# A Fourier mixing and low-rank mixer kernel on one core: one sum of the second batch's fold taken in the opening, one of the third batch's loads issued after the second batch's narrow sums, and the third batch's fold three slots later

## The chip, the core and the metric

The kernel runs on one core of a Trainium2 chip. A core has five engines, each with a queue of its own that it works through in order: TensorE (PE) multiplies matrices, VectorE (DVE) and ScalarE (ACT) do elementwise work, GpSimd (POOL) does elementwise work and issues DMAs, and SyncE (SP) issues DMAs. An instruction that waits for a semaphore holds up everything behind it on its engine. TensorE writes its products to PSUM, from where VectorE or ScalarE must take them ("evict" them) before the buffer can be used again; all other tiles lie in SBUF.

The metric is the device time in microseconds (us) of one execution.

## The reference

```
x: 8 x 3136 x 256 float32
X  = fft(fft(x, axis=1), axis=2).real          # along the sequence, then along the channels
h  = X.transpose(0, 2, 1) @ U @ V              # U: 3136 x 32, V: 32 x 3136
u  = X + h.transpose(0, 2, 1)
out = u + relu(u @ w_ch1) @ w_ch2              # w_ch1: 256 x 1024, w_ch2: 1024 x 256
```

## The kernel before

**Tiling.** A batch has 3136 rows. Both transforms are products with tables of sines and cosines, and the symmetries of the tables are used to fold the input before the products. Rows are laid on 99 partitions times 8 tiles, in two halves (`a` = 0, 1). `xf` holds the rows forward, `xr` the rows that mirror them, both float32, and both exist once: batch b + 1 is loaded into them when batch b's fold has read them.

**The fold of a batch** (`fold`, line 402) is VectorE's work. For each half and for `xr` and `xf`, `along_d` (line 382) takes the difference (part 0) and then the sum (part 1) of mirrored channels, 99 x 1024 elements each, into the bf16 tiles `EOR_` and `EOF_` (`eor` and `eof` in the profile); `alone` (line 390) copies the channel without a partner on GpSimd for the first two batches. `mirror` (line 394) joins forward and mirrored rows to `EOS` (`eos`). When both halves are done, `half` (line 398) makes the two tiles `G[par]` (`g`), which the products read. `load_half(b + 1, a)` (line 106) stands in the fold behind the four sums of half a: a gather of `xf`, a load of `xr` and two loads of single rows, all four issued by GpSimd.

**The sequence transform.** `seq` (line 470) multiplies `G` with the tables, 425 columns at a time, of which the last 32 belong to U. Its products are called `pt`, or `pth` and `ptq` where `halves` and `quarters` use more symmetry; ScalarE copies one part (`ev`, `ex`), VectorE adds and subtracts into `A` and `B` (128 x 1569). `first_channel` and `narrow` (lines 547 and 626) do the same for channel 0 alone: products `ptc`, two copies by ScalarE (`evc`, `evo`), and for the second batch sums and two mirrored copies (`turn_row`, line 632) on GpSimd, which fill row 32 of `VA[1]`. In the opening, for batch 0, the same sums go to GpSimd and VectorE, and their last parts are kept in the list `late` (line 590).

**The channel transform.** `even_ch` and `odd_ch` (lines 650 and 659) multiply `A` and `B` (products `pst`); ScalarE copies the first (`evd`), VectorE forms `S` and `T`. Batch 0 does it with `chan` (line 640).

**The low-rank part.** `joined` (line 680) finishes the tile `TAB` (`tab`) on GpSimd, `lowrank` (line 690) multiplies it (`ptt`), and ScalarE copies the result to `TA[b]` (`ta`).

**The chunks.** The output is made in 49 chunks of 512 rows. `front(c)` (line 727) makes `u` for a chunk: products `ph` of `TA` and `VA`, to which VectorE adds `S` or `T`. Chunk 3 and chunk 6 are cut in two pieces, and the larger piece of chunk 6 is the first of the second batch. SyncE transposes `u` to `ut` by DMA. `first_product` (line 744) has eight steps j for each chunk: two products of 512 columns (L750) and a relu by ScalarE to `h` (L752), with three PSUM buffers. `second_product` (line 754) of the chunk before runs in between: 32 products of 256 columns (L766) for each chunk, with two PSUM buffers, and VectorE adds `ut` to `o` (L772 to L775), which SyncE stores.

**What sets the order.** Up to the second chunk the order is written out by hand. The main loop (line 1035) counts slots, eight to a chunk, and the dictionary `due` (line 1000) says in which slot which step of the other stages is written; `spread` distributes a list of steps over a range of slots. Batch b's range is counted back from `hi` (line 1010): 42 for the second batch, 90 for the third, 138 for the fourth. From the second chunk on (line 1037) a planner puts the instructions in each engine's queue by its own estimate of when they can run, where dependencies allow it; only the instructions given to `pin` (line 377) keep the order in which they are written. What the planner made of a kernel is fixed when it is built: the chip follows it even where the times are other than the planner took them.

Of the kernel before, what the change touches and what calls it, by code (L numbers as in the profile page):

```python
# [16 lines left out]
P = 128  # L17
PQ = 98
KP = PQ + 1
NI = 8  # L20
# [7 lines left out]
def kernel(  # L28
# [9 lines left out]
    nc = tc.nc  # L38
    B, S, D = x.shape
# [25 lines left out]
    xr = cpool.tile([KP, 2, NI, D], FP32, name="xr")  # L65

    def load_f(b, a):
        gather(xf[:PQ, a].rearrange("p i d -> p (i d)"), x, B * S // 8 - 1,
               xidx[:PQ, b, a:a + 1], 8 * D, D)
# [36 lines left out]
    def load_half(b, a):  # L106
        load_f(b, a)
        load_r(b, a)
        load_0(b, a, nc.gpsimd)
# [56 lines left out]
    EOR_ = cpool.tile([KP, 2, NI, 258], BF16, name="eor")  # L166
# [212 lines left out]
        if PIN:  # L379
            tc.keep_in_program_order(ins)  # L380

    def along_d(a, src, dst, part):
        v = src[:, a, :, P:]
        lo, hi = (bass.AP(v.tensor, v.offset, [v.ap[0], v.ap[1], [s, 2], [2 * s, QD]])
                  for s in (-1, 1))
        pin(nc.vector.tensor_tensor(  # L386
            dst[:, a, :, part * P:(part + 1) * P].rearrange("p i (k t) -> p i k t", k=2), lo, hi,
            op=AL.subtract if part == 0 else AL.add))

    def alone(a, src, dst):  # L390

        pin(nc.gpsimd.tensor_copy(dst[:, a, :, 256:257], src[:, a, :, 0:1]))
# [5 lines left out]
    def half(b, par, cols):  # L398
        pin(nc.vector.tensor_tensor(G[b % 2][par][:, :, cols], EOS[:, 0, :, cols],  # L399
                                    EOS[:, 1, :, cols], op=AL.add if par == 0 else AL.subtract))  # L400

    def fold(b):

        for a in range(2):
            for src, dst in ((xr, EOR_), (xf, EOF_)) if b == 1 else ((xf, EOF_), (xr, EOR_)):
                if b < B0:
                    yield lambda a=a, src=src, dst=dst: (alone(a, src, dst),
                                                         along_d(a, src, dst, 0))
                else:
                    yield lambda a=a, src=src, dst=dst: along_d(a, src, dst, 0)  # L410
                yield lambda a=a, src=src, dst=dst: along_d(a, src, dst, 1)
            if b + 1 < B:
                yield lambda a=a: load_half(b + 1, a)
            yield lambda a=a: mirror(a, slice(0, 128), AL.subtract)
            yield lambda a=a: mirror(a, slice(128, 258 if b < B0 else 256), AL.add)
        for par in range(2):
            yield lambda par=par: half(b, par, slice(0, 258 if b < B0 else 256))
# [92 lines left out]
    B0 = 2  # L510
# [83 lines left out]
    def column_steps():  # L594
# [5 lines left out]
        def lower(t):  # L600
            with tc.issue_after(LAST[0].ins):
                nc.scalar.copy(cb[t][:], (cf, cr)[t][:])
# [23 lines left out]
    def first_channel(b, **kw):  # L626
        dst = VA[b][R:R + 1]
        yield from narrow(1, lambda par, i: G[b][par][:kp(i), i, 256:256 + R], dst,
                          tc1 if b else TF[:1, 0], tr1[:] if b else None, **kw)
        mid = (HALF + S) // 2  # L630
        for lo, hi in ((HALF + 1, mid), (mid, S)):
            def turn_row(lo=lo, hi=hi):
                if b:
                    nc.gpsimd.tensor_copy(dst[:, lo:hi], dst[:, S - lo:S - hi:-1])
                    return
                with tc.issue_after(LAST[0].ins):
                    nc.scalar.copy(dst[:, lo:hi], dst[:, S - lo:S - hi:-1])
            yield turn_row
# [29 lines left out]
    def across(b, ch, back):  # L668
# [3 lines left out]
        hi = (ch + 1) * 392 + 1  # L672
        with tc.issue_after(LAST[0].ins):
            if back:
# [15 lines left out]
    def lowrank(b, tag=("dft", 3)):  # L690
        pt = psum.tile([P, 256], FP32, tag=tag[0], name="ptt", bufs=tag[1])
        for typ in range(2):
            nc.tensor.matmul(pt[:], TAB[:, typ * R:typ * R + P], MDT[typ][:], start=(typ == 0),
                             stop=(typ == 1))
        nc.scalar.copy(TA[b % 2][:R, :], pt[:R])
# [48 lines left out]
    def first_product(c, j):  # L744
# [4 lines left out]
        for s in range(2):  # L749
            nc.tensor.matmul(p1[:], W1[:, s, j::JT], k["u"][:, s, :],  # L750
                             start=(s == 0), stop=(s == 1))
        LAST[0] = nc.scalar.activation(k["h"][:, j, :], p1[:], AF.Relu)  # L752

# [31 lines left out]
    def sequence(b):  # L785

        for par in range(2):
            for typ in (1, 0):
                for pn in range(2):
                    yield lambda par=par, typ=typ, pn=pn: seq(b, par, typ, pn)  # L790
# [6 lines left out]

    CK = {}
    ST = {}
    LAST = [None]  # L800

    for t in tabs:
        nc.vector.memset(t[:, :, :, 0:1], 0.0)
# [154 lines left out]
    late = []  # L958
# [3 lines left out]
    seq(0, 0, 1, 0)  # L962
    narrow_0[1]()
    ta_rows(1)
    late[1]()
    late.append(seq(0, 0, 1, 1))
    pu = [psum.tile([P, CH], FP32, tag="p1", name="pu0", bufs=3) for _ in range(2)]

    def straight(k, start):

        for h in range(2):
            nc.tensor.matmul(pu[h][:], (MC, MSN)[k][:, h * P:(h + 1) * P],
                             ST[0]["AB"[k]][:, :CH], start=start, stop=False)

    late.append(seq(0, 1, 1, 0) or seq(0, 1, 1, 1))
    straight(1, True)
    lowrank(0, ("p2", 2))
    straight(0, False)
    tc.no_sync_barrier()
    setup.close()  # L980
# [8 lines left out]
    def piece(n, h, **kw):  # L989
        return [lambda: chan(0, cuts[n], cuts[n + 1], h, dve=h == 1 and n in (1, 2), **kw)]  # L990

    for step in piece(1, 0) + piece(1, 1, tag=("p2", 2)) + late[2:] + late[:1]:
        step()
    column_zeros()
    nc.gpsimd.tensor_copy(ME[:], MC[:, :P])
# [4 lines left out]
    due = {2: piece(2, 0), 3: piece(2, 1), 8: piece(3, 0),  # L1000
           9: piece(3, 1), 10: piece(0, 0), 11: piece(0, 1), 13: [lambda: last_row(0)],
           16: narrow_0[3:4], 18: narrow_0[4:5]}

    def spread(steps, lo, hi):

        for n, step in enumerate(steps):
            due.setdefault(lo + (hi - lo) * n // len(steps), []).append(step)

    for b in range(1, B):
        hi = 8 * (b * S // CH - 1) + 2  # L1010
        if b == 1:
            steps = list(fold(b))
            spread(steps[:1], 2, 3)
            spread(steps[1:], 4, 21)
            row = list(first_channel(b))
            spread(list(sequence(b)), 23, hi - 5)
            spread(row[:1], 25, 26)
            spread(row[1:], 26, 29)
            due.setdefault(hi - 5, []).append(lambda b=b: joined(b))
            due.setdefault(hi - 3, []).append(lambda b=b: lowrank(b))  # L1020
            for n, step in zip((-5, -4, -2, -1, 3, 5, 8, 11), channels(b)):
                due.setdefault(hi + n, []).append(step)
            continue
        first, second = (66, 35) if b > B0 else (64, 32)
        spread(list(fold(b)), hi - first, hi - second)
        steps = [*sequence(b), *channels(b)]
        last = steps.pop()
        spread([*steps, lambda b=b, last=last: (last(), joined(b), row_in(b)),
                lambda b=b: lowrank(b)], hi - min(second, 33), hi)
        if b == B0:  # L1030
            for at, step in zip((28, 27, 25, 24, 23, 22, 20), column_steps()):
                due.setdefault(hi - at, []).append(step)
    for n, step in enumerate(column_loads()):
        due.setdefault(8 + 44 * n // 28, []).append(step)
# [44 lines left out]
```

## Time and profile before

| What | Value |
|---|---|
| Median of three runs | 447.29 us (446.68 to 447.43) |
| The profiled execution's own time | 447.18 us |
| Its span (first to last instruction) | 445.3 us |
| TensorE busy, matmuls | 437.1 us |
| TensorE busy, weight loads (beside the matmuls) | 317.1 us |
| VectorE busy | 353.8 us |
| ScalarE busy | 300.4 us |
| GpSimd busy | 86.2 us |
| TensorE clock granted, every stage of 10 us but the last | 1.00 |

How to read the lines. In a line of the timeline the first two numbers are the start and the length in us; then come the engine, the line of the kernel, the operation, the tile written and the tiles read, the shapes, and how many instructions the line stands for. What stands in brackets is how long the engine sat idle before it, and what it waited for. In a line of a stage ("50.00:60.00") the stage's length is followed by the busy time and the count of instructions of PE, PE's weight loads, DVE, ACT and POOL, then the granted clock, the DMA engines' share and GB/s. A matmul's end is modelled: the next one can start well before it. On VectorE and ScalarE, too, an instruction's length overlaps a little with the next one's, so the distance of two starts (here called the step) is the cost of one more.

### The profile page before, as it was taken

To read this page: it belongs to the slowest core of one execution; us is meant where nothing else is said; L and a number is where in the kernel's file an instruction comes from. 1 tells how busy PE (TensorE), PEld (TensorE's weight loads), DVE (VectorE), ACT (ScalarE), POOL (GpSimd) and SP (SyncE) were. 2 spreads that over 40 slices of the span, in tenths; PEclk is the share of its full clock that TensorE was granted. 3 is DMA by queue.
4 is the path that set the end of the run, shared out by engine and by line. 5 is a ranking of instruction groups with operands and counts; after the bars stand their busy time and mean duration, and the time that the engine had idled before them with its cause. 6 is when DMAs were issued, how large, how long until landed. Compare 5 with 4: busy or idle time off the path is not lost.

```text
span 445.3 us, 8146 instructions
## 1 busy us (share of the span) xinstructions
PE 437.1 (98%) x3004; PEld 317.1 (71%) x3004; DVE 353.8 (79%) x846; ACT 300.4 (67%) x570; POOL 86.2 (19%) x148
## 2 busy tenths in 40 slices
PE   8999899999999999999999999999999999999996
PEld 6556666777677777777777777777777777777775
DVE  8879979997998799878998799878998776343433
ACT  8867657866776569655876568655876569656562
POOL 8984264203521011300211011300000000000000
PEclk9999999999999999999999999999999999999999
DMA  7998979992689437672669437782343433435252
GB/s 133 208 232 131 265 125 211 159 211 72 154 208 225 109 96 218 195 167 76 163 193 227 110 94 216 190 173 76 90 119 95 101 90 79 121 87 131 83 135 102
DMA packets 103249, 65.36 MB, mean 147 GB/s; under 512 B 73806, under 2 KB 99624, under 8 KB 100464
## 3 DMA queue, kind: packets, MB, share of 16 engines
q1 hardware_dynamic: 97528, 39.10, 39.3%
q0 software_dynamic: 5664, 25.75, 21.9%
q8 instruction: 23, 0.38, 0.4%
q14 instruction: 16, 0.13, 0.1%
q10 hardware_dynamic: 18, 0.00, 0.0%
HBM read 29.33 MB, written 25.69 MB: 124 GB/s over the span
## 4 chain that ended last, share of the span: by engine, by line
PE 85%; DVE 8%; DMA 2%; ACT 2%; issue 1%; POOL 1%; DVEq 0%; POOLq 0%
PE p L766 35%; PE p L750 34%; PE pt L485 5%; PE ph L724 4%; DMA xb<-in_x_dram,xidx 2%; PE ptq L446 2%; DVE eof L386 2%; DVE eor L386 1%; PE pst L655 1%; PE pst L664 1%; ACT h L752 1%; DVE u L740 1%; PE m L856 1%; PE ptc L557 1%; DVE g L399 1%
## 5 line engine op out<-in xcount | busy, mean ns | idle before, releaser
L752 ACT ACTIVATE h<-p 128x512 bf16<-128x512 f32 x392 | 221.2, 597 | 119.9 <-PE p L750 117.7
L750 PE MATMUL p<-u,w 128*128 128x512 bf16 x784 | 217.8, 380 | 1.4 <-DVE u L740 1.2
L766 PE MATMUL p<-w,h 128*128 128x256 bf16 x1568 | 203.2, 273 | 0.0
L766 PEld LDWEIGHTS <-h 128*128 128x128 bf16 x1568 | 153.1, 98 | 51.2 <-issue 1.0
L750 PEld LDWEIGHTS <-w 128*128 128x128 bf16 x784 | 106.5, 144 | 36.2 <-DVE u L740 1.5
L772 DVE TENSOR_TENSOR o<-p,ut 128x4 f32<-128x4 f32 (+1 forms) x100 | 16.1, 161 | 53.9 <-PE p L766 52.4
L774 DVE TENSOR_TENSOR o<-p,ut 128x254 f32<-128x254 f32 (+1 forms) x100 | 40.5, 405 | 0.0
L775 DVE TENSOR_TENSOR o<-p,ut 128x254 f32<-128x254 f32 (+1 forms) x100 | 40.5, 405 | 0.0
L386 DVE TENSOR_TENSOR eof<-xf 99x1024 bf16<-99x1024 f32 x28 | 34.6, 1253 | 0.0
L740 DVE TENSOR_TENSOR u<-ph,S 128x512 bf16<-128x512 f32 (+23 forms) x63 | 34.2, 552 | 0.0
L740 DVE TENSOR_TENSOR u<-ph,T 128x512 bf16<-128x512 f32 (+23 forms) x63 | 34.2, 553 | 0.0
L386 DVE TENSOR_TENSOR eor<-xr 99x1024 bf16<-99x1024 f32 x28 | 33.9, 1214 | 0.0
L468 POOL TENSOR_TENSOR tab<-tf 128x64 bf16<-128x64 f32 x7 | 2.2, 316 | 153.6 <-DVE tf L492 153.6
L55 POOL DMA_INDIRECT xf<-in_x_dram,xidx x14 | 18.5, 1324 | 68.6 <-DVE eof L386 57.9
L724 PE MATMUL ph<-va,ta 128*128 128x512 bf16 (+16 forms) x126 | 29.0, 328 | 0.5 <-DVE ev L437 0.3
L485 PEld LDWEIGHTS <-g 98*128 98x128 bf16 (+1 forms) x144 | 13.9, 98 | 11.9 <-issue 0.7
L666 DVE TENSOR_TENSOR S<-evd,pst 128x392 bf16<-128x392 f32 (+1 forms) x28 | 15.7, 560 | 6.5 <-PE pst L664 4.1
L395 DVE TENSOR_TENSOR eos<-eof,eor 99x1024 bf16<-99x1024 bf16 (+1 forms) x28 | 18.6, 682 | 0.0
L457 DVE TENSOR_TENSOR ev<-ptq,ex 128x131 f32<-128x131 f32 (+1 forms) x24 | 7.0, 290 | 13.0 <-ACT ex L450 12.9
L399 DVE TENSOR_TENSOR g<-eos 99x2048 bf16<-99x2048 bf16 (+1 forms) x14 | 17.1, 1218 | 0.0
L485 PE MATMUL pt<-tabs,g 98*128 98x425 bf16 x72 | 15.8, 344 | 0.0
L485 PE MATMUL pt<-tabc,g 98*128 98x425 bf16 x72 | 15.7, 344 | 0.0
(208 smaller groups left out, 386.4 us busy)
## 6 DMA issues: line engine op xcount, KB each, us to landing
out_dram<-o SPq DMA_DIRECT2D x48, 512.0 KB
xr<-in_x_dram POOLq DMA_DIRECT2D x14, 784.0 KB, 8.0
xb<-in_x_dram POOLq DMA_DIRECT2D x2, 392.0 KB, 6.6
ut<-u SPq DMA_TRANSPOSE x49
w<-in_moe_w_ch_dram POOLq DMA_DIRECT2D x1, 512.0 KB, 10.1
out_dram<-o SPq DMA_DIRECT2D x4, 128.0 KB
va<-in_moe_V_dram POOLq DMA_DIRECT2D x2, 196.0 KB, 7.9
w<-in_moe_w_ch_dram POOLq DMA_DIRECT2D x1, 256.0 KB, 6.9
```

The lines of the kernel that those rows point to most:

```text
L55: nc.gpsimd.indirect_dma_start(out_, None, bass.AP(t.tensor, t.offset, [[w, rows], [1, w]]), bass.IndirectOffsetOnAxis(idx, 0), element_of ...
L386: pin(nc.vector.tensor_tensor(dst[:, a, :, part * P:(part + 1) * P].rearrange("p i (k t) -> p i k t", k=2), lo, hi, op=AL.subtract if part ...
L395: pin(nc.vector.tensor_tensor(EOS[:, a, :, cols], EOF_[:, a, :, cols], EOR_[:, a, ::-1][:, :, cols], op=op))
L399: pin(nc.vector.tensor_tensor(G[b % 2][par][:, :, cols], EOS[:, 0, :, cols], EOS[:, 1, :, cols], op=AL.add if par == 0 else AL.subtract))
L485: nc.tensor.matmul(pt[:], g[:kp(i), i, P * typ:P * (typ + 1)], tabs[typ][:kp(i), i, par, :], start=(n == 0), stop=(n == NI // 2 - 1))
L724: nc.tensor.matmul(ph, TA[b % 2][:k, s * P:(s + 1) * P], VA[b % 2][:k, lo:hi], start=start, stop=True)
L740: nc.vector.tensor_tensor(u[:, s, col:col + hi - lo], ph[:, col:col + hi - lo], src, op=AL.add)
L750: nc.tensor.matmul(p1[:], W1[:, s, j::JT], k["u"][:, s, :], start=(s == 0), stop=(s == 1))
L752: LAST[0] = nc.scalar.activation(k["h"][:, j, :], p1[:], AF.Relu)
L766: nc.tensor.matmul(p2[:, t % w, :], h[:, j, rs], W2[:, j, :], start=(j == 0), stop=(j == JT - 1))
L774: nc.vector.tensor_tensor(o[:, ts, 1:P], p2[:, :w, 1:P], ut[:, ts, 1:P], op=AL.add)
L775: nc.vector.tensor_tensor(o[:, ts, P + 1:D], p2[:, :w, P + 1:D], ut[:, tT, P - 1:0:-1], op=AL.add)
```

## The change

Three things are changed.

- `along_d` can take some of its eight row tiles. For the second batch the first sum (`xr`, half 0, part 0) is done for six of the eight in the opening, between batch 0's `lowrank` product and the chunk-0 product that follows it; in the fold only the other two are left. The last part of batch 0's narrow sum on GpSimd (`late[1]`) is written later, behind the first pieces of the channel transform.
- The load of the third batch's second half no longer stands in the second batch's fold. It is written in slot 30, behind the second of the narrow row's mirrored copies on GpSimd (`LAST[1]`).
- Slots: the second batch's fold runs to slot 23 instead of 21, with two steps instead of one in slot 2; its sequence products and narrow sums begin one slot earlier. The third batch's fold goes from slots 26 to 58 to slots 29 to 60, its column steps two slots earlier, and the fourth batch's fold begins two slots earlier.

```diff
-    def along_d(a, src, dst, part):
-        v = src[:, a, :, P:]
+    def along_d(a, src, dst, part, lo_i=0, hi_i=NI):
+        v = src[:, a, lo_i:hi_i, P:]
...
-            dst[:, a, :, part * P:(part + 1) * P].rearrange("p i (k t) -> p i k t", k=2), lo, hi,
+            dst[:, a, lo_i:hi_i, part * P:(part + 1) * P].rearrange("p i (k t) -> p i k t", k=2),
+            lo, hi,
...
+    AHEAD = 6
+
     def fold(b):
...
                 if b < B0:
-                    yield lambda a=a, src=src, dst=dst: (alone(a, src, dst),
-                                                         along_d(a, src, dst, 0))
+                    ahead = AHEAD if a == 0 and src is xr else 0
+                    yield lambda a=a, src=src, dst=dst, ahead=ahead: (
+                        alone(a, src, dst), along_d(a, src, dst, 0, ahead))
...
-            if b + 1 < B:
+            if b + 1 < B and (b >= B0 or a == 0):
                 yield lambda a=a: load_half(b + 1, a)
...
-                    nc.gpsimd.tensor_copy(dst[:, lo:hi], dst[:, S - lo:S - hi:-1])
+                    LAST[1] = nc.gpsimd.tensor_copy(dst[:, lo:hi], dst[:, S - lo:S - hi:-1])
...
     ta_rows(1)
-    late[1]()
     late.append(seq(0, 0, 1, 1))
...
     lowrank(0, ("p2", 2))
+    along_d(0, xr, EOR_, 0, 0, AHEAD)
     straight(0, False)
...
-    for step in piece(1, 0) + piece(1, 1, tag=("p2", 2)) + late[2:] + late[:1]:
+    for step in piece(1, 0) + piece(1, 1, tag=("p2", 2)) + late[2:] + late[1::-1]:
...
             steps = list(fold(b))
-            spread(steps[:1], 2, 3)
-            spread(steps[1:], 4, 21)
+            spread(steps[:2], 2, 3)
+            spread(steps[2:], 4, 23)
             row = list(first_channel(b))
-            spread(list(sequence(b)), 23, hi - 5)
-            spread(row[:1], 25, 26)
-            spread(row[1:], 26, 29)
+            spread(list(sequence(b)), 22, hi - 5)
+            spread(row[:1], 24, 25)
+            spread(row[1:], 25, 28)
+
+            def load_last(b=b):
+                with tc.issue_after(LAST[1].ins):
+                    load_half(b + 1, 1)
+            due.setdefault(30, []).append(load_last)
...
-        first, second = (66, 35) if b > B0 else (64, 32)
+        first, second = (61, 30) if b == B0 else (66 + 2 * (b == B0 + 1), 35)
         spread(list(fold(b)), hi - first, hi - second)
...
-            for at, step in zip((28, 27, 25, 24, 23, 22, 20), column_steps()):
+            for at, step in zip((30, 29, 27, 26, 25, 24, 22), column_steps()):
```

More of the change, by code (lines that the diff above doesn't have):

```diff
@@ L799 @@
     ST = {}
-    LAST = [None]
+    LAST = [None, None]
     for t in tabs:
```

## The prediction

> **What bounds the kernel.** I read the busy shares and the chain of waits on the page first, then the engines' busy time by stage, then TensorE's order of time around each hole in it.
>
> ```profile
> PE 437.1 (98%) x3004; PEld 317.1 (71%) x3004; DVE 353.8 (79%) x846; ACT 300.4 (67%) x570; POOL 86.2 (19%) x148
> PE 85%; DVE 8%; DMA 2%; ACT 2%; issue 1%; POOL 1%; DVEq 0%; POOLq 0%
> ...
> 50.00:60.00 10.00, 8.79 (x73) 6.03 (x72) 7.68 (x19) 5.53 (x12) 2.31 (x4) 1.00 0.96 201
> ...
> 210.00:220.00 10.00, 10.00 (x68) 7.17 (x67) 9.49 (x22) 7.53 (x15) 2.11 (x4) 1.00 0.45 125
> ```
>
> TensorE carries 85% of the chain, and in the later batches (210 to 220) it has no hole at all. The change keeps its products, so only its holes between 30 and 120 us can be won, and every new one is paid in full. They are these, each named by its releaser:
>
> ```profile
> 66.06 1.03 PE L750 MATMUL p<-u,w 128*128 128x512 bf16 x4
> ...
> 52.41 0.56 PE L430 MATMUL pth<-tabc,g 98*128 98x229 bf16 x4
> 54.19 0.43 PE L750 MATMUL p<-u,w 128*128 128x512 bf16 x1 [1.22 <-DVE u L740]
> ...
> 63.63 0.56 PE L430 MATMUL pth<-tabc,g 98*128 98x229 bf16 x4 [0.29 <-DVE u L740]
> ...
> 72.25 0.38 PE L724 MATMUL ph<-va,ta 65*128 65x512 bf16 x1 [0.34 <-DVE ev L437]
> ...
> 79.78 0.38 PE L724 MATMUL ph<-va,ta 65*128 65x64 bf16 x2 [0.17 <-ACT ta L695]
> ...
> 117.21 0.33 PE L655 MATMUL pst<-A,me 128*128 128x392 bf16 x1 [0.48 <-DVE T L666]
> ```
>
> Four 512-column products span 1.03 and one lasts 0.38, so they start 0.217 apart; by columns, 256 cost 0.109 and 392 cost 0.166. A shown hole of i therefore loses i + 0.16: 1.38, 0.45, 0.50, 0.33 and 0.64, 3.30 us in all. That is nearly everything the change could win behind the opening.
>
> **The sum taken in the opening.** VectorE had this gap and these durations:
>
> ```profile
> 30.53 0.69 DVE L985 CAST u<-pu 128x512 bf16<-128x512 f32 x1 [1.17 <-PE pu L724]
> ...
> 33.23 1.23 DVE L386 TENSOR_TENSOR eor<-xr 99x1024 bf16<-99x1024 f32 x1
> 34.49 0.57 DVE L647 CAST T<-pst 128x392 bf16<-128x392 f32 x1
> ...
> 35.24 1.44 PE L750 MATMUL p<-u,w 128*128 128x512 bf16 x5
> ...
> 36.17 1.22 DVE L386 TENSOR_TENSOR eor<-xr 99x1024 bf16<-99x1024 f32 x1
> ...
> 83.89 2.35 DVE L386 TENSOR_TENSOR eor<-xr 99x1024 bf16<-99x1024 f32 x2
> ```
>
> Two sums take 2.35, so one costs a step of 1.13; six of its eight rows are some 0.9 (by size) and fit the 1.17 gap if the data is there.
>
> ```profile
> 17.09 0.57 POOL L86 DMA_DIRECT2D xr<-in_x_dram  x1
> ...
> xr<-in_x_dram POOLq DMA_DIRECT2D x1, 784.0 KB, 11.0
> ```
>
> It lands at 28.1, 1.2 us before the gap opens at 29.36: free. But the built order puts the remaining quarter (0.3) and the whole second sum (1.13) ahead of T and both u of chunk 1, where one sum (1.26 from 33.23 to 34.49) stood. So u ends 0.17 later. TensorE was waiting for it: five products from 35.24 took 1.44, against 1.25 without a hole (four times 0.217 and 0.38). **+0.17.** The deferred sum of the narrow row keeps its place in GpSimd's queue and ahead of u's wait: 0.
>
> **Chunk 3's u ahead of the two g.** In the built order VectorE now evicts u of chunk 3 before it makes G, and TensorE runs four L750 and two L766 before the first pth.
>
> ```profile
> 39.79 1.04 PE L766 MATMUL p<-w,h 128*128 128x256 bf16 x8
> ...
> 50.43 1.23 DVE L399 TENSOR_TENSOR g<-eos 99x2064 bf16<-99x2064 bf16 x1
> 51.58 0.41 DVE L774 TENSOR_TENSOR o<-p,ut 128x254 f32<-128x254 f32 x1
> ...
> 53.39 0.18 DVE L740 TENSOR_TENSOR u<-ph,S 128x33 bf16<-128x33 f32 x1
> ...
> 54.71 0.15 DVE L772 TENSOR_TENSOR o<-p,ut 128x4 f32<-128x4 f32 x1
> ```
>
> From 36.17 to 53.39 VectorE had no gap: 17.22. Of this 1.13 is now done earlier and two g (1.15 each, 50.43 to 51.58) stand behind: 13.79 from 36.34. Some of the gain is lost at once: the first o now comes up at 39.8, but its matmuls end at 40.83, or 41.1 with the shift and a handover, a wait of 1.27. So u starts at 51.40 and ends at 52.72 (1.32, as from 53.39 to 54.71). TensorE arrives at 52.58 and needs the last part at 52.80: the 1.38 goes. The first g ends near 53.95, TensorE reaches pth at 53.67: 0.3 comes back. **-1.08.**
>
> **Folds and GpSimd's queue.** Before:
>
> ```profile
> 58.88 0.24 POOL L582 TENSOR_TENSOR tc<-evo,evc 1x32 f32<-1x32 f32 x1 [7.63 <-ACT evo L569]
> 60.40 1.85 DVE L386 TENSOR_TENSOR eof<-xf 99x1024 bf16<-99x1024 f32 x1
> 64.91 2.60 POOL L634 COPY va<-va 1x784 bf16<-1x784 bf16 x2
> 65.16 1.66 DVE L386 TENSOR_TENSOR eof<-xf 99x1024 bf16<-99x1024 f32 x1
> 73.42 0.20 POOL L683 COPY tab<-tr 1x32 bf16<-1x32 bf16 x1
> ```
>
> The narrow sums waited 7.63 for ScalarE's copy, not for the load ahead of them, so moving the load's four DMAs behind them starts nothing sooner; it only puts eight issues in a row before the tab copy, which on my layout still comes near 73. The load is issued when GpSimd's copies end, at 67.5 at the latest, and lands by 79 (at 11.0); its reader, a fold sum, now stands near 86. The 0.45 before the third pth was a wait for chunk 4's u, which stood on VectorE behind the eof of 1.85. The third batch's fold now begins three slots later, both of its first sums stand behind that u, and pth finds its buffer free: **-0.45**. One fold sum meets GpSimd's copies as before (1.66 against 1.22) and still holds up the product that found 0.50: I leave it, between 0 and 1.0. On SyncE one transpose goes ahead of two column loads, with no reader near: 0.
>
> [...]
>
> **The new hole.** The lowrank product of the second batch, which everything of chunk 6 needs, moves 54 products back in TensorE's order. In the built program it stands so:
>
> ```
> L770 p2 (chunk 5) x16, then x13   [u of chunk 5 used up]
> L697 ptt x2; L659, L668 pst; L770 x1
> L728 ph 64, 448 [waits TA]; L770 x2; L728 ph 64, 448 [waits evd]
> L659 pst [waits DVE T]; L668 pst [waits evd of it]
> L754 x3 [waits DVE u S, behind an eof]; pst; L754 x3 [waits u T]
> ```
>
> Before, 17 L766 and eight L750 lay between ptt and chunk 6's first L750; now three L766 do. The 54 products that went ahead (46 L766, eight L750) take 6.75, and TensorE is 1.36 earlier by the terms above, so ptt comes at 84.2 instead of 78.78. The links:
>
> ```profile
> 78.78 0.27 PE L693 MATMUL ptt<-msn,tab 128*128 128x256 bf16 x1
> ...
> 79.38 0.35 ACT L695 CAST ta<-ptt 32x256 bf16<-32x256 f32 x1
> 79.64 0.48 ACT L657 COPY evd<-pst 128x392 f32<-128x392 f32 x1
> ...
> 82.57 0.21 DVE L740 TENSOR_TENSOR u<-ph,T 128x64 bf16<-128x64 f32 x1
> 82.70 0.74 DVE L740 TENSOR_TENSOR u<-ph,S 128x448 bf16<-128x448 f32 x2
> 83.36 0.61 DVE L740 TENSOR_TENSOR u<-ph,T 128x448 bf16<-128x448 f32 x1
> ...
> 86.89 0.55 DVE L666 TENSOR_TENSOR S<-evd,pst 128x392 bf16<-128x392 f32 x1
> 87.36 0.56 DVE L666 TENSOR_TENSOR T<-evd,pst 128x392 bf16<-128x392 f32 x1
> ...
> 87.94 0.60 ACT L752 ACTIVATE h<-p 128x512 bf16<-128x512 f32 x1
> 88.73 1.08 ACT L752 ACTIVATE h<-p 128x512 bf16<-128x512 f32 x2 [0.20 <-PE p L750]
> 89.84 0.51 ACT L676 COPY va<-A 64x391 bf16<-64x391 bf16 x1
> ```
>
> From ptt's start (0), 0.05 per handover: products done 0.38, ta 0.78, ph from 0.83 to 1.05; evd 0.68 to 1.16; second ph to 1.49. VectorE: u 64 at 1.26, S 1.39, T 1.86 to 2.42; eof to 3.46; u S to 4.07; u T to 4.73. TensorE: pst at 2.47 (hole 0.98), its evd to 3.32, next pst 3.37 (0.73), L754 at 4.12 (0.58), with 0.17 before ph: 2.46. Then chunk 6's products run almost without L766 between them, and each pair waits for one of three PSUM buffers: ScalarE has an evd, eight h (0.48 apart: 1.08 less 0.60) and two va copies, some 5.3 us without a rest. The first three h end at 6.20, 6.68 and 7.17, the next, behind a va copy, at 8.1, 8.6 and 9.1, the last two at 10.0 and 10.5. The fourth pair waits for the first h, and so on: holes of 0.22, 0.05, 0.06 and 0.17, then 0.54 where an L766 needs the seventh h, and 0.2 at chunk 7's fourth pair, 1.24 in all. **+3.70** together (2.46 and 1.24), which takes the place of the 0.33 at 79.78 (**-0.33**). Behind it TensorE is late and the third batch's S and T are on time: the 0.64 goes (**-0.64**).
>
> **Sum.** 0.17 - 1.08 - 0.45 + 3.70 - 0.33 - 0.64 = +1.37. The profiled execution took 447.18 (span 445.3, 1.88 around it), 0.11 under the median of 447.29: **448.6**. Ends: the hole 2.46 if ScalarE keeps up, 4.33 if the eof inside it takes 1.85; the gains 0.5 more (the hole left alone), or less by that and the 0.64. That is -0.4 to +3.1 around 447.18, 446.8 to 450.3; for eight in ten 447.2 to 450.0.
>
> **Rivals.** *The lowrank chain is covered* (the other side): its place is ptt to chunk 6's first L754, its price 3.70, and below 1.4 of it the kernel is faster by over 0.2%. With 0.33 as before: 445.2. For it: tab is ready 10 us ahead. Against it: TensorE's order is fixed, with three L766 left. 0.08. *Chain at its low end*, 2.46 with all gains: 447.3, no change; for it, ScalarE is busy for only 67% of the span; 0.19. *The early sum waits for its load*: if xr lands 2.7 us later than 28.1, the sum (0.9) ends at 31.7 and holds up chunk 0's u by 1.2, so 449.8; against it, the margin of 1.2; 0.04. *The clock falls in the hole*: half speed for as long as it takes from ptt to L754 (4.1) adds 2.0: 450.6; against it, the hole of 1.22 at 53 left the clock at 1.00 and no piece here is longer; 0.03.
> [...]
>
> **Chances.** Forecast 0.66, rivals 0.08, 0.19, 0.04, 0.03. About 0.2% (0.9 us) is what a measurement of this kernel can tell from no change. Faster 0.08; within 0.2% 0.20; slower 0.72.
>
> **What would show it.** Right: VectorE's first eor near 29.4 with six rows; L754 of chunk 3 without a hole near 52.6; ptt near 84 with holes of some 0.5 to 1.0 behind it, released by T, evd and u; no hole near 117. Wrong: ptt followed by L754 without holes, or new holes after 120.

## The result, and the profile after

| Kernel | Median of its runs | Lowest and highest |
|---|---|---|
| before | 447.25 us (6 runs) | 446.43 to 448.27 |
| after | 453.22 us (6 runs) | 451.72 to 455.99 |

The changed kernel is slower: 1.0138 times the time before, interval 1.0104 to 1.0171. The forecast had the direction right and the size wrong: 448.6, with 450.0 as the upper end. The profiled execution took 451.72 (span 449.5) and is the shortest of the six.

The first part of the page of the changed kernel:

```profile
PE 438.8 (98%) x3004; PEld 315.8 (70%) x3004; DVE 353.6 (79%) x847; ACT 300.3 (67%) x570; POOL 84.0 (19%) x148
```

TensorE's busy time is 1.7 longer than before and the span 4.2, so more than half of the loss is idle time. Two stages of 10 us hold it. As before, the columns of a stage are its length, the busy time and count of PE, PE's weight loads, DVE, ACT and POOL, then the clock, the DMA engines' share and GB/s.

```profile
80.00:90.00 10.00, 7.42 (x57) 5.46 (x55) 5.45 (x14) 2.66 (x6) 0.00 (x0) 0.99 0.67 111
90.00:100.00 10.00, 9.69 (x46) 5.40 (x45) 10.00 (x16) 7.86 (x15) 3.35 (x4) 0.84 1.01 220
```

In the first stage TensorE is busy for 7.42 of 10, and VectorE, which it waits for, for only 5.45. In the second the clock is 0.84.

The timeline of the changed kernel, all engines, around ptt:

```profile
84.10 0.27 PE L697 MATMUL ptt<-msn,tab 128*128 128x256 bf16 x1
...
85.37 0.17 DVE L776 TENSOR_TENSOR o<-p,ut 128x4 f32<-128x4 f32 x1 [3.41 <-PE ph L728]
...
86.11 0.21 DVE L744 TENSOR_TENSOR u<-ph,T 128x64 bf16<-128x64 f32 x1
...
87.32 0.33 PE L659 MATMUL pst<-A,me 128*128 128x392 bf16 x1 [1.56 <-DVE T L670]
...
88.22 0.33 PE L668 MATMUL pst<-B,msn 128*128 128x392 bf16 x1 [0.57 <-ACT evd L661]
...
88.98 0.81 PE L754 MATMUL p<-u,w 128*128 128x512 bf16 x3 [0.44 <-DVE u L744]
...
89.86 1.49 PE L754 MATMUL p<-u,w 128*128 128x512 bf16 x3
...
92.00 1.81 PE L754 MATMUL p<-u,w 128*128 128x512 bf16 x5
```

ptt comes at 84.10, where the forecast put it (84.2). That is partly luck: the opening lost more than forecast, but this execution's products had begun 0.67 earlier than those of the one before (in 3, 5 and 7 ptt comes at 84.80 to 85.12). Measured from start to start, the holes behind it are 0.17, 1.73, 0.73 and 0.60, 3.23 together (forecast 2.46); the 1.73 stood in the forecast as 0.98. An o stands ahead of u on VectorE: it waited for 3.41. The row names `ph`, which this o does not read; what it waited for is a transpose on SyncE (in 3 and 7 the row of the same o names the transpose itself). SyncE's own rows:

```profile
68.20 9.04 SPq L545 DMA_DIRECT2D cr<-in_x_dram  x2
77.34 6.08 SPq L722 DMA_TRANSPOSE ut<-u  x1
83.46 1.70 SPq L545 DMA_DIRECT2D cr<-in_x_dram  x2
```

Two column loads that elsewhere take 1.70 held SyncE for 9.04, and the transpose behind them, of chunk 5's u, for 6.08. By the semaphore updates in the trace it landed at 85.29, 0.08 before the o started. Then the clock fell: the three products from 89.86 and the five from 92.00 start 0.427 apart instead of 0.217. Seven such steps (the two `ph` between them included) lose 1.47; what ScalarE still holds up later is 0.39 and 0.26.

In the opening, where the forecast had +0.17:

```profile
28.59 0.95 DVE L386 TENSOR_TENSOR eor<-xr 99x768 bf16<-99x768 f32 x1
...
28.85 1.42 POOL L590 TENSOR_TENSOR va<-eo 1x392 bf16<-1x392 f32 x1
...
30.30 0.58 ACT L989 CAST u<-pu 128x512 bf16<-128x512 f32 x1 [1.26 <-POOL va L590]
...
30.94 1.46 PE L754 MATMUL p<-u,w 128*128 128x512 bf16 x6 [0.70 <-ACT u L989]
```

The early sum has its data in time, but GpSimd's sum beside it takes 1.42 instead of 0.87 (29.52 before), both u of chunk 0 wait for GpSimd, and the hole ahead of the first L754 grows from 0.32 to 0.87.

The other steps, in TensorE's timeline:

```profile
52.51 1.03 PE L754 MATMUL p<-u,w 128*128 128x512 bf16 x4
...
53.92 0.56 PE L434 MATMUL pth<-tabc,g 98*128 98x229 bf16 x4 [0.17 <-DVE g L400]
...
69.95 0.39 PE L728 MATMUL ph<-va,ta 65*128 65x512 bf16 x1 [0.42 <-DVE ev L441]
...
131.37 0.33 PE L668 MATMUL pst<-B,msn 128*128 128x392 bf16 x1 [0.58 <-ACT evd L661]
```

Chunk 3's products start without a hole and 0.33 comes back at pth (forecast 0.3); the third pth waits no more; the hole that was left alone is 0.58. Only the third batch still loses 0.74, at 130 now instead of 0.65 at 116.

### The profile page after: what moved, and what is told of

Read it like the earlier page. It is cut to its first block, busy times and chain, and to the rows that moved or that the text cites. A ratio compares the mean times of both kernels' runs of the same rounds, so it can differ in the third digit from the quotient of the medians.

```text
span 449.5 us, 8148 instructions
## 1 busy us (share of the span) xinstructions
PE 438.8 (98%) x3004; PEld 315.8 (70%) x3004; DVE 353.6 (79%) x847; ACT 300.3 (67%) x570; POOL 84.0 (19%) x148
## 4 chain that ended last, share of the span: by engine, by line
PE 86%; DVE 5%; ACT 5%; issue 2%; POOL 1%; ACTq 0%; DVEq 0%
PE p L770 35%; PE p L754 35%; PE pt L489 5%; PE ph L728 4%; PE ptq L450 2%; ACT h L756 1%; ACT tabs L238 1%; PE pst L668 1%; PE pst L659 1%; DVE eof L386 1%; DVE u L744 1%; PE m L860 1%; DVE eor L386 1%; PE ptc L561 1%; ACT tabc L357 1%
## 5 line engine op out<-in xcount | busy, mean ns | idle before, releaser
L754 PE MATMUL p<-u,w 128*128 128x512 bf16 x784 | 217.7, 381 | 1.4 <-ACT u L989 0.7
L754 PEld LDWEIGHTS <-w 128*128 128x128 bf16 x784 | 106.6, 144 | 37.8 <-issue 4.8
L386 DVE TENSOR_TENSOR eor<-xr 99x1024 bf16<-99x1024 f32 (+2 forms) x29 | 34.0, 1179 | 0.0
L661 ACT COPY evd<-pst 128x392 f32<-128x392 f32 (+1 forms) x28 | 13.5, 482 | 4.4 <-PE pst L659 4.4
```

The costliest lines, as they stand in the source:

```text
L386: pin(nc.vector.tensor_tensor(dst[:, a, lo_i:hi_i, part * P:(part + 1) * P].rearrange("p i (k t) -> p i k t", k=2), lo, hi, op=AL.subtract ...
L754: nc.tensor.matmul(p1[:], W1[:, s, j::JT], k["u"][:, s, :], start=(s == 0), stop=(s == 1))
```

## The experiments

Each group of four ran on one chip with the kernel before beside it: 447.56 for the first four (17 runs), 447.50 for the second (17), 447.46 for the last (35). Diffs are against the changed kernel unless said otherwise.

**1. ptt early, the load where the change put it.**

```diff
-            due.setdefault(hi - 5, []).append(lambda b=b: joined(b))
+            due.setdefault(hi - 7, []).append(lambda b=b: joined(b))
```

> The changed kernel with joined (GpSimd's two tab instructions) two slots earlier, so that they stand ahead of the last four of the eight DMA issues; in the built order ptt then stands at product 463 instead of 533 of TensorE. Theory (the loss is the uncovered lowrank chain, with what follows it): the holes of 80 to 98 us (3.54 + 2.04 lost in these 20 us of the changed kernel's trace) go, the gains at chunk 3 (1.08) and at the third pth (0.45) stay, so 446 to 447, at or under the kernel before. Rival 1 (the loss is from the moved load itself, its transfers beside others, not from ptt's place): at least 451. Rival 2 (only the clock's fall matters, and it comes wherever ptt stands): 449 to 451, with products of 512 starting 0.427 apart somewhere in 70 to 100.

Measured: 451.83 (1.0121, 1.0079 to 1.0163). The holes behind ptt are gone, and the time is not: one hole of 3.71 at 96.7 has taken their place. Rival 1 holds, the moved load has a cost of its own. The clock fell here too, but only behind that hole (four steps of 0.427 from 101.46), and the time is over the 449 to 451 of rival 2. All engines' timeline of this kernel, around that hole:

```profile
83.68 1.73 POOL L55 DMA_INDIRECT xf<-in_x_dram,xidx  x1 [7.57 <-DVE eof L386]
...
87.85 7.97 SPq L722 DMA_TRANSPOSE ut<-u  x1
...
92.04 2.35 DVE L400 TENSOR_TENSOR g<-eos 99x2048 bf16<-99x2048 bf16 x2
...
99.08 0.17 DVE L776 TENSOR_TENSOR o<-p,ut 128x4 f32<-128x4 f32 x1 [4.69 <-issue]
...
100.55 1.12 PE L489 MATMUL pt<-tabc,g 98*128 98x425 bf16 x4 [3.54 <-DVE u L744]
```

It is the same wait one chunk later. Chunk 6's transpose goes out at 87.85, behind the load of the fourth batch's second half (from 83.68). It lands at 99.00, the o at 99.08 had waited for it, and u and TensorE stood behind that o.

**2. The load back in the fold, all else kept.**

```diff
-            if b + 1 < B and (b >= B0 or a == 0):
+            if b + 1 < B:
...
-            due.setdefault(30, []).append(load_last)
```

> The changed kernel with the third batch's second load back in the second batch's fold; everything else of the change kept. In the built order ptt then stands at product 484, as before the change. Theory: 446 to 447.5, as the run with the tab instructions moved. Rival (the third batch's later fold or the opening make the loss): 450 or more.

Measured: 446.49 (0.9977, 0.9963 to 0.9991; 12 runs), and this is faster than either kernel. The move of the load makes the whole loss; the rest of the change is worth 1.07. In this kernel the two column loads and the two transposes behind them hold SyncE only shortly (2.01, 4.04 and 4.14 in the kernel before), and ptt stands at 78.80:

```profile
69.56 1.92 SPq L545 DMA_DIRECT2D cr<-in_x_dram  x2
74.44 1.27 SPq L722 DMA_TRANSPOSE ut<-u  x1
...
83.83 1.26 SPq L722 DMA_TRANSPOSE ut<-u  x1
```

**3. Without the sum in the opening.**

```diff
-    AHEAD = 6
+    AHEAD = 0
...
+    late[1]()
     late.append(seq(0, 0, 1, 1))
...
-    along_d(0, xr, EOR_, 0, 0, AHEAD)
...
-    for step in piece(1, 0) + piece(1, 1, tag=("p2", 2)) + late[2:] + late[1::-1]:
+    for step in piece(1, 0) + piece(1, 1, tag=("p2", 2)) + late[2:] + late[:1]:
```

> The changed kernel without the sum in the opening, the late part of batch 0's narrow sum in its old place. Theory: the opening's holes (0.87 at 29.96, 0.38 at 35.82) fall back to 0.32 and 0.16, 0.77 won, but the 1.13 of VectorE's work stands in the run up to chunk 3's u again, and the hole at 52.7 comes back with some 0.9: within 0.5 of the changed kernel. Rival (as predicted, the opening costs 0.17 alone): 0.7 slower than the changed kernel.

Measured: 453.43 (1.0149, 1.0123 to 1.0175), 0.2 from the changed kernel: the early sum is worth nothing that can be measured. But the reason I had given is wrong. The opening's first hole is 0.32 again, chunk 3 has no hole either (0.32 at pth), and the sum is paid at 35.6, where two full sums now stand ahead of chunk 1's u. VectorE's and TensorE's rows of this kernel:

```profile
33.20 2.37 DVE L386 TENSOR_TENSOR eor<-xr 99x1024 bf16<-99x1024 f32 x2
35.60 0.57 DVE L651 CAST T<-pst 128x392 bf16<-128x392 f32 x1
...
36.82 0.44 PE L754 MATMUL p<-u,w 128*128 128x512 bf16 x1 [0.80 <-ACT h L756]
...
85.31 0.17 DVE L776 TENSOR_TENSOR o<-p,ut 128x4 f32<-128x4 f32 x1 [2.34 <-DMA ut<-u]
...
87.60 0.33 PE L659 MATMUL pst<-A,me 128*128 128x392 bf16 x1 [0.82 <-DVE T L670]
```

The hole at 36 is 0.97 from start to start, against 0.15 with the early sum. (The row names an h that ended at the same moment; the first u of chunk 1 ends 0.06 ahead of this product, at 36.76, as it does in the changed kernel, at 35.76.)

The last two rows stand behind ptt, which comes at 85.12 here. The load is whole and chunk 5's transpose lands at 85.23, about as late as in the changed kernel, and the o waits for it. Yet the hole of 1.73 is 0.98 here: chunk 6's first u, due 1.25 behind the later ptt, found VectorE free.

**4. The third batch's fold back in its old slots.**

```diff
-        first, second = (61, 30) if b == B0 else (66 + 2 * (b == B0 + 1), 35)
+        first, second = (66, 35) if b > B0 else (64, 32)
...
-            for at, step in zip((30, 29, 27, 26, 25, 24, 22), column_steps()):
+            for at, step in zip((28, 27, 25, 24, 23, 22, 20), column_steps()):
```

> The changed kernel with the third batch's fold and column steps, and the fourth's fold, back in their old slots. ptt stays at product 533. Theory: the loss stays, 452.5 to 454; 0.45 comes back at the third pth. Rival (the later fold put SyncE's transpose and VectorE's o ahead of chunk 6's u): the 1.73 hole shrinks to 1.0 and the time falls by 0.7 or more, and with a shorter stretch the clock does not fall: 450 or less.

Measured: 456.89 (1.0204, 1.0174 to 1.0235), worse than both expected. With the load moved, the later fold had not made the loss, it had softened it. With the fold earlier the next load follows the moved one at once (70.99 behind 68.03), and the transpose of chunk 5 takes SyncE 14.82. All engines' timeline:

```profile
72.02 0.59 POOL L86 DMA_DIRECT2D xr<-in_x_dram  x1
...
73.48 14.82 SPq L722 DMA_TRANSPOSE ut<-u  x1
...
84.84 5.00 PE L770 MATMUL p<-w,h 128*128 128x256 bf16 x29 [3.08 <-DVE o L779]
...
89.90 0.17 DVE L776 TENSOR_TENSOR o<-p,ut 128x4 f32<-128x4 f32 x1 [4.39 <-issue]
```

**5. A tenth of the moved load's data.**

```diff
     def load_half(b, a):
-        load_f(b, a)
-        load_r(b, a)
+        if (b, a) == (2, 1):
+            gather(xf[:8, a].rearrange("p i d -> p (i d)"), x, B * S // 8 - 1,
+                   xidx[:8, b, a:a + 1], 8 * D, D)
+            nc.gpsimd.dma_start(out=xr[:8, a].rearrange("p i d -> p (i d)"),
+                                in_=bass.AP(x.tensor, rev(x, b, a, D).offset, [[8 * D, 8], [1, 8 * D]]))
+        else:
+            load_f(b, a)
+            load_r(b, a)
```

> The changed kernel with the third batch's second load cut to 8 of its 98 partitions (gather and mirrored rows; the other 90 keep what the batch before left, so the third batch's second half is wrong). The same DMAs are issued at the same places, and ptt stays at product 533. Theory (two costs: ptt's late place, and two half loads back to back that crowd the DMA engines, so that SyncE's two column loads at 68 take 9.04 instead of 1.92 and the transpose behind them 6.08 instead of 1.27): with a tenth of the data the column loads and the transpose are short again, the o at 82 to 85 waits no more, the 1.73 hole falls to about 1.0, the clock stays up, and the time is 448.5 to 450, what ptt's place alone costs. Rival (data does not matter, the place of ptt makes the whole loss): 452 to 454.

Measured: 451.60 (1.0090, 1.0070 to 1.0109). The transfers are as expected, the time is between the two. SyncE's two column loads take 1.74, the transpose 1.27 and it lands at 80.37 instead of 85.29; the hole of 1.73 is 0.98, to the hundredth what the forecast's chain gave. But 3 and 7 have the same 0.98 with the whole load. From all engines' timeline:

```profile
74.67 1.27 SPq L728 DMA_TRANSPOSE ut<-u  x1
...
87.28 0.33 PE L665 MATMUL pst<-A,me 128*128 128x392 bf16 x1 [0.82 <-DVE T L676]
```

The clock fell all the same in the profiled run (seven steps of 0.427 and one of 0.406). Of its four runs the two with a mean clock of 1.00 took 450.90 and 451.48, the two with 0.995 and 0.996 took 451.72 and 452.26: the fall costs about 0.8 here. By the medians the data of the load, against the changed kernel, costs 1.6; the profiled executions of the two, 451.72 each, do not show it.

**6. Both: a tenth of the data, and ptt early.** The edits of 1 and 5 together.

> The same cut of the load together with the tab instructions two slots earlier (ptt at product 463, as in e1). Theory of two costs: both are gone, 446 to 447.2, as with the load in its old place (446.5), and no hole of 3.7 at 96.7. Rival (the 3.7 of e1 come from the order of the instructions): 451 as e1.

Measured: 455.59 (1.0152, 1.0112 to 1.0191), against my theory: the hole at 96.7 is there and 9.5 long. It was not made by the moved load's data. Chunk 6's transpose is issued at 86.67, again behind the next load (from 83.64), and lands at 104.75; the o behind it waited for 10.48. So in this kernel and in 1 the costly neighbour is the load of the fourth batch's second half, which is issued ahead of that transpose there (in 2 the transpose goes out first, at 83.83 against 85.25, and lands at 86.90).

**7. Without the column loads on SyncE.**

```diff
-    for n, step in enumerate(column_loads()):
-        due.setdefault(8 + 44 * n // 28, []).append(step)
```

> The changed kernel without any of the loads of channel 0's columns on SyncE (channel 0 of the last six batches is then computed from zeros). ptt stays at product 533. If the bulk loads alone crowd the DMA engines: the transpose at 77 still takes 4 or more, 451 or more. If the many small packets of the column loads are what stands ahead of the transpose and slows it: the transpose is issued right after its u, at 74, takes 1.3 to 2, and the time is 448.5 to 450, as with the cut load.

Measured: 451.09 (1.0081, 1.0060 to 1.0103), the first branch. The transpose is now issued at 74.83, 2.5 earlier than in the changed kernel, and still lands only at 84.34, behind the load in flight (83.98). The bulk loads alone delay it. Yet the time is 2.1 under the changed kernel's, and the hole behind ptt is 0.98: the o waited 1.59 for the transpose and was through before u, which ptt at 84.97 left at 86.22. A late landing alone does not make the hole.

**8. The load back, and the late part of the narrow sum in its old place.** Against the kernel of 2:

```diff
     ta_rows(1)
+    late[1]()
...
-    for step in piece(1, 0) + piece(1, 1, tag=("p2", 2)) + late[2:] + late[1::-1]:
+    for step in piece(1, 0) + piece(1, 1, tag=("p2", 2)) + late[2:] + late[:1]:
```

> The changed kernel with the load in the second batch's fold again (e2, 446.49) and the late part of batch 0's narrow sum back in its old place, so that GpSimd is through with it before VectorE's early sum. Theory (the sum and GpSimd's 1.42 instead of 0.87 get in each other's way, and both u of chunk 0 wait for GpSimd): the hole at 30.7 falls from 0.87 to 0.3, 445.9. Rival (GpSimd's work costs the same wherever it stands in the opening, or the product before it waits instead): 446.5, no change from e2.

Measured: 446.52 (0.9983, 0.9955 to 1.0010), and the hole is 0.87 as in 2. The edit moves the line in the text and no instruction in any queue: GpSimd reaches it behind the fills of ta either way. It is a repeat of 2 and says nothing on the collision, and it shows that this part of the change does nothing.

**9. and 10. ptt late, all loads where the kernel of 2 has them.** Five fills of a free tile on GpSimd, and in 10 two, between its load and the tab instructions. Against the kernel of 2:

```diff
-        q.dma_start(out=xr[PQ:KP, a].rearrange("p i d -> p (i d)"),
+        LAST[1] = q.dma_start(out=xr[PQ:KP, a].rearrange("p i d -> p (i d)"),
...
-                    LAST[1] = nc.gpsimd.tensor_copy(dst[:, lo:hi], dst[:, S - lo:S - hi:-1])
+                    nc.gpsimd.tensor_copy(dst[:, lo:hi], dst[:, S - lo:S - hi:-1])
...
+        if b == 1:
+            for _ in range(5):
+                with tc.issue_after(LAST[1].ins):
+                    LAST[1] = nc.gpsimd.memset(rows[:].bitcast(I32), 0)
+        with tc.issue_after(LAST[1].ins):
-        join_t(nc.gpsimd)
+            join_t(nc.gpsimd)
...
```

> The kernel of e2 (load back in its old place, 446.5), with five fills of a free tile on GpSimd between its last load and the tab instructions, and nothing else. The planner then puts ptt at product 536 (484 in e2, 533 in the changed kernel), while all loads stay where e2 has them. Theory (ptt's late place alone makes most of the loss): the serial holes of about 1.0, 0.7 and 0.6 and what follows are there, 450 to 451.5. Rival (the place costs only together with the moved load's transfers): under 447.5. My predicted sum for the place alone (+3.70 less 0.33): 449.9.

> As e9 with two fills: ptt at product 503, with 14 L770 between ptt and chunk 6's first product. Theory: the chain of about 4.7 is covered by some 1.5 of products, the later holes stay in part: 447.5 to 449.5, between e2 and e9. Rival: 446.5 as e2 or as e9 (a switch and not a slope).

Measured: 450.29 with ptt at product 536 (1.0055, 1.0029 to 1.0080), 448.86 at 503 (1.0029, 1.0002 to 1.0056), 446.49 at 484. The late place alone costs 3.8, and it is no switch: it rises from the first 19 products on. All engines' timeline of 9 shows the chain as the forecast had drawn it:

```profile
85.21 0.27 PE L702 MATMUL ptt<-msn,tab 128*128 128x256 bf16 x1
...
86.45 0.23 DVE L749 TENSOR_TENSOR u<-ph,T 128x64 bf16<-128x64 f32 x1 [0.23 <-PE ph L733]
...
87.68 0.33 PE L659 MATMUL pst<-A,me 128*128 128x392 bf16 x1 [0.89 <-DVE T L670]
...
88.58 0.33 PE L668 MATMUL pst<-B,msn 128*128 128x392 bf16 x1 [0.57 <-ACT evd L661]
...
89.34 0.81 PE L759 MATMUL p<-u,w 128*128 128x512 bf16 x2 [0.44 <-DVE u L749]
```

Its holes are 0.28, 1.05, 0.73, 0.60, and then, paced by ScalarE, 0.30, 0.35 and 0.26: 3.57, where the forecast had 3.70. The hole of the third batch is halved here (0.32 at 122, forecast to go); what the change had at 130 is not there.

**11. As 1, with the third batch's fold three slots later still.**

```diff
-        first, second = (61, 30) if b == B0 else (66 + 2 * (b == B0 + 1), 35)
+        first, second = (58, 27) if b == B0 else (66 + 2 * (b == B0 + 1), 35)
```

> The kernel of e1 (tab instructions two slots earlier, load still moved; 451.83, one hole of 3.71 at 96.7) with the third batch's fold another three slots later, so that the load of the fourth batch's second half is issued later. Theory (a transpose issued behind a bulk load lands only when the load has landed: 99.0 behind 97.0 in e1, and the o that waits for it holds up VectorE): if the transpose of chunk 6 now goes ahead of that load it lands in about 3, the hole of 3.7 goes, 446.5 to 448. Rival (the hole comes from the order of the fold): 451 or more.

Measured: 449.92, from 447.44 to 455.01 in ten runs (1.0023, 0.9992 to 1.0054). Not decided. In the profiled run (453.10) chunk 6's transpose was still behind the load: issued at 89.64 against 86.36, landed at 98.65 against 97.73, and TensorE lost 2.67 at 98. The four runs with a clock of 1.00 took 447.4 to 448.7, as expected of a transpose that goes ahead; they have no trace, so that it went ahead in them is not shown.

**12. The load back, GpSimd's narrow sum earlier.** Against the kernel of 2:

```diff
+    late[1]()
     ta_rows(1)
...
-    for step in piece(1, 0) + piece(1, 1, tag=("p2", 2)) + late[2:] + late[1::-1]:
+    for step in piece(1, 0) + piece(1, 1, tag=("p2", 2)) + late[2:] + late[:1]:
```

> The kernel of e2 with the late part of batch 0's narrow sum ahead of the fills of ta on GpSimd (the edit of e8 left every engine's order as it was). Theory (GpSimd's sum takes 1.42 instead of 0.87 beside VectorE's early sum, and both u of chunk 0 wait for it): it now starts near 28.0 and is through by 29.2, the hole of 0.87 falls to 0.3, 446.0. Rival (another wait takes its place): 446.5.

Measured: 446.80 (0.9974, 0.9952 to 0.9996), no change from 2; the rival holds. All engines' timeline:

```profile
27.92 0.87 POOL L590 TENSOR_TENSOR va<-eo 1x392 bf16<-1x392 f32 x1
27.93 0.93 DVE L472 TENSOR_TENSOR tab<-tf 128x64 bf16<-128x64 f32 x1
...
28.92 0.28 PE L697 MATMUL ptt<-msn,tab 128*128 128x256 bf16 x1 [0.96 <-DVE tab L472]
```

The hole at the first L754 is 0.27, as expected, and a hole of 1.12 ahead of ptt has taken its place (0.41 elsewhere): VectorE's short add for batch 0's tab, 0.23 elsewhere, now takes 0.93, beside GpSimd's sum of 0.87 that started 0.01 earlier.

**The transposes side by side.** Issue and last landing, by the semaphore updates in the traces (us); the last column is when the bulk load that was in flight at the issue had landed.

```
kernel   transpose issued   landed   took    load landed
after          62.08         65.18    3.10   none in flight
before         75.13         82.18    7.05   81.35
2              74.44         81.45    7.01   80.51
5              74.67         80.37    5.70   79.66
after          77.34         85.29    7.95   83.12
1              87.85         99.00   11.15   96.48
4              73.48         89.83   16.34   89.31
6              86.67        104.75   18.08   91.17; its second part, issued 0.91 later, 104.57
```

From 36 to 125 us the fourteen traces tell the landing of 126 transposes. Of these, 54 were issued with such a load in flight for at least another 0.3 us: 52 landed behind it, after 3.7 to 18.1 us. The two others were issued within 1 us of a gather (91.81 in the changed kernel, landed 98.40, the gather at 102.03; and one in 3). The 72 others took 3.0 to 4.6. The kernel before has late transposes too (75.13 and 84.96, landed after 7.05 and 9.37) and loses nothing behind them.

## Why the forecast was right and wrong

| Step of the forecast | Forecast | Profile after |
|---|---|---|
| opening | +0.17 | +0.81 (holes of 0.74 became 1.55) |
| chunk 3's u | -1.08 | -1.05 (1.38 became 0.33) |
| third pth | -0.45 | -0.45 |
| hole left alone | 0 | +0.08 |
| lowrank hole, less the 0.33 | +3.37 | +5.01 (3.23 in the chain, 1.47 clock, 0.65 ScalarE, less 0.34) |
| third batch's S and T | -0.64 | +0.27 (0.74 and 0.18 for 0.65) |
| a hole at 353 | none | +0.28 |
| sum | +1.37 | +4.95 |

The span grew by 4.2; the rest is the start, where the same products (pu) came 0.67 earlier in this execution than in the one before (27.62 against 28.29). Other traces have starts near either of the two. Of the 3.58 by which the profile exceeds the forecast, 1.64 lies in the lowrank hole (0.77 in the chain, and clock and ScalarE at 2.12 where ScalarE alone had 1.24), 0.91 in the third batch's S and T and 0.64 in the opening. The median of the six runs is another 1.5 above this execution.

**What was right.** The gains at chunk 3 and at the third pth, and above all the new hole: that the planner's order puts ptt late, that the chain behind it is uncovered, and what this costs. Run alone (9 against 2) it costs 3.8 where the forecast had 3.37; its profile has 3.57 of holes against 3.70.

**The step that failed** is the one that costed the moved load and SyncE's queue at nothing: "it only puts eight issues in a row before the tab copy" and "On SyncE one transpose goes ahead of two column loads, with no reader near: 0". Beside ptt's late place the move costs 2.9 by the medians (453.22 against 450.29 in 9, where ptt is as late and all loads are in their old places; 3.7 by the ratios).

What of this the traces show: the eight issues are two half loads back to back. With them in flight the column loads hold SyncE (two of them for 9.04, against 1.92 in 2), chunk 5's transpose goes out 2.2 later than before (77.34 against 75.13) and lands late, and it does have a reader near: the o of chunk 5, which stands on VectorE ahead of chunk 6's u. In the profiled execution u came 2.01 behind ptt and not 1.26 as the chain assumed, and 0.75 was lost. The other part is the 0.74 at 130, which the profiles of the changed kernel, 3, 5 and 7 have and those of 2 and 9 have not. A new hole after 120 was one of the forecast's own signs of being wrong.

What stays open: the 0.75 depends on when ptt comes. In 3 and 7 the transpose is as late or nearly so (landed at 85.23 and 84.34), the o waits for it (2.34 and 1.59), and the hole is 0.98 as in 5, because ptt comes 0.9 to 1.0 later. The profiled executions of the changed kernel, 3, 5 and 7 took 451.72, 451.59, 451.72 and 451.52; what sets the medians of the first two (453.22, 453.43) apart from those of 5 and 7 (451.60, 451.09) happened in executions without a trace. So the price of the moved load is measured, and its path only in part. The forecast dated each load's landing and never asked what else was to go over the DMA engines meanwhile.

**The clock.** The rival "the clock falls in the hole" had 0.03, because no piece was longer than the 1.22 that had left the clock alone. In the trace it fell with pieces of 1.73, 0.73 and 0.60 between short products. The seven long steps lose 1.47, but ScalarE then holds up less: 0.65, where 3 and 7, whose clock did not fall, have 1.62. So the fall costs some 0.5 to 0.8 (0.8 by two runs of 5 against two). It does not tell the long runs from the short ones: the two runs of the changed kernel with a mean clock of 0.999 and 1.000 took 453.13 and 453.92.

The length of one piece does not decide it: with the same three holes (0.98, 0.73, 0.60) the clock fell in the profile of 5 (mean 0.995) and not in that of 3 (mean 0.999). In the changed kernel the trace's record of the granted clock has 0.50 from 89.72 to 93.13, for 3.41, and TensorE was idle for 2.35 of the 3.41 ahead of it (86.30 to 89.72; idle is the distance of two starts less the product's own step). In 5 the clock was 0.67 in the stage from 90 to 95, in 1 it was 0.66 from 100 to 105. In 9, with holes of 0.28, 1.05, 0.73 and 0.60, it stayed at 1.00 from 80 to 100. What decides it is not shown: no run tested it. The forecast's reason, that no piece was longer than one that had left the clock alone, gave the wrong answer.

**Smaller terms.** The opening: the deferred sum kept its place in GpSimd's queue, as forecast, and not its length. Beside VectorE's sum of 0.95 GpSimd's took 1.42 instead of 0.87: the gap on VectorE was not free of GpSimd. 12 only moves the 0.7 from one wait to another. The 0.64 of the third batch: forecast to vanish because TensorE would be late, it came back at 130 behind an evd. In 9, where ptt is as late, 0.32 is left at 122 and nothing at 130, and 3, 5 and 7 have the 0.74; that it belongs to the order that the load's move makes is argued from this, not shown.

**The account.** From 447.3: the change without the load's move -1.1 (2), ptt's late place +3.8 (9), what is left of the move with a tenth of the data +1.3 (5 against 9; its profile has 0.75 at 130 and 0.20 at 119 where 9 has 0.32 at 122, and its clock fell), the load's data +1.6 (after against 5): 452.9 of the measured 453.2. By the intervals each of these can be off by up to 1.1, and the split of the last two is a difference of medians that no trace bears out. What stays open is the spread: the runs of the changed kernel and of 1, 3, 4, 6 and 11 lie 4.3 to 7.6 apart, those of 5, 7 and 9 under 1.6. The wide ones all have the load moved (as 5 and 7 have), but single long runs are found elsewhere too (453.42 in 8), and what the long ones lose was not traced.

## What to carry to other kernels

Before a load is moved, list what else goes through the DMA engines until it lands and which reader of those transfers stands ahead of others in an engine's queue: in the profiled execution a late transpose held up an o for 3.41, and the o held up u behind it, by 0.75. Where a planner sets the order, an issue costs more than its time on the queue: eight of them ahead of a step of 0.5 us moved the step's consumer 49 products back (533 against 484 in 2), although on the chip the step ran at the same 73.4, so a small, urgent step belongs ahead of bulk issues. And run the parts of a change alone: all of this one but the load were together a gain of 1.1.

## What was unexpected of the hardware

- A DMA transpose that took 3.0 to 4.6 us without a bulk load in flight landed only behind the load in flight in 52 of 54 cases of these traces, after up to 18.1 us. It held SyncE's queue meanwhile for 14.82 us at the most (in 4).
- A tensor_tensor on VectorE took longer beside one on GpSimd, and the reverse: in 12 VectorE's took 0.93 instead of 0.23 beside a GpSimd sum of 0.87 that had started 0.01 earlier, and in the changed kernel GpSimd's took 1.42 instead of 0.87 beside a VectorE sum of 0.95 that had started 0.26 earlier. Why is not shown.
- TensorE's clock halved for 3.41 us in the changed kernel with no idle piece over 1.73 before it, and it fell in 5 with none over 0.98. In 3, with the same three holes as in 5, it did not fall.
